# GEGLU after hash attention: weights staged in fp32 and cast on GpSimd, pair 0 in half-pair pieces, pairs 2 to 5 transposed by DMA

## Chip, cores and metric

One Trainium2 chip, one core of it. The metric is the device time of one execution in microseconds. The kernel before was run six times; an execution taken by the hardware profiler gives the trace that all stage times below come from.

## What is computed

Attention over 4 batches, 8 heads, 768 tokens and a head size of 64, in which a query sees only keys of the same hash bucket (six signs of a random projection), followed by a gated MLP on the heads laid side by side (512 columns):

```python
q_bits = np.einsum('bhsd,dk->bhsk', q, proj) > 0          # k_bits alike; six bits a token
mask = q_bucket[:, :, :, None] == k_bucket[:, :, None, :]
scores = np.where(mask, scale * q @ k.T, -1e9)
attn = softmax(scores) @ v                                # [4, 8, 768, 64]
x = attn.transpose(0, 2, 1, 3).reshape(B * S, H * D)      # [3072, 512]
ffn = (gelu(x @ w_gate) * (x @ w_val)) @ w_out            # d_ff = 1536
out = x + sigmoid(x @ w_res) * ffn
```

All inputs and the output are fp32; the kernel multiplies in bf16, and hashes in fp32.

## The kernel before

**Pairs, chunks and slots.** Heads go in pairs: 16 pairs, four to a batch. The scores of a pair are cut into nine chunks of 1024 columns (line 311): each has blocks of 128 keys by 512 or 2 x 256 queries for both heads. One chunk is one slot, and the main loop at line 575 has 144 of them. A slot issues the score matmuls of its chunk (`scores`, line 374) into one of two PSUM buffers `sp`, then ScalarE's exponential into `e` (line 378), then the tasks hung on that slot by `at(slot, f, ...)`, then in batches 1 to 3 some MLP matmuls as filler, and last the value matmuls of an earlier chunk (`flush`, `values`, line 355). The order on every engine is that of the program; nothing is reordered by a scheduler.

**Masks as extra rows.** Seven extra rows of q and k carry the hash bits, so that unequal buckets give a large negative score. The first head of a pair uses rows 0 to 71 of the transposed tile `aug`; the second head uses the tile `second`, whose rows 64 to 127 are a copy of `aug`'s (`move_second`, line 192, GpSimd) and whose rows 0 to 6 are the mask rows. Rows 7 to 63 are zero. The preparation of a pair is: `load` (line 88, SP's queue) of q, k and v in fp32; `cast` to bf16 (lines 175 to 179); a transpose on PE (line 200) with a copy out of PSUM (lines 206 and 208) or by DMA (line 187); `blocks` (line 212), VectorE's 32x32 transposes of the fp32 tile for the hash; `hash_half` (line 248, fp32 matmuls, then bits at line 253); `spread` (lines 261 and 268), which puts the bits in rows; and the mask rows. Pair 0's are copied in place by VectorE and ScalarE (`spread_in_place`, line 281); all others are moved by four small DMAs (`mask_rows`, line 290). `values_prep` (lines 293 to 308, GpSimd) casts v and sums it over the blocks of keys.

**Where each pair is prepared.** Pair 0 and most of pair 1 come ahead of slot 0 (lines 470 to 503). Pairs 2 and 3 are prepared in slots 1 to 14, transposed on PE, hashed together (two halves of 384 columns). From pair 4 on, two pairs are prepared at a time in the 18 slots before they are needed, transposed by DMA.

**The MLP.** In the fourth slot of the next batch (`LEAD = 4`), `gate_val` (line 383) computes 12 blocks of 128 hidden columns: eight matmuls with `wg`, GELU on ScalarE (line 399), eight with `wv`, a product on VectorE (line 402). `project` (line 407) is the filler of the rest of the batch: `wr` and tanh (lines 415 and 418), `wo` (line 425), the end on VectorE and GpSimd (lines 430 and 432). A planner gives each slot of batches 1 to 3 so many filler matmuls that PE's load is even; batch 0 has no filler.

**The weights.** `load_w` (line 162) issues a DMA on GpSimd that reads fp32 and writes bf16. The weights come in 12 pieces: eight quarters of `wg` and `wv`, `wr`, and three thirds of `wo`. Four are issued in slots 17 to 20, the other eight in slot 39, just ahead of the first gate stage.

## Time and profile before

| what | us |
|---|---|
| median of six runs (lowest to highest) | 363.06 (361.79 to 364.22) |
| the profiled execution | 363.67 |
| its span in the trace | 361.9 |
| first exponential starts | 12.75 |
| gate matmuls of batch 0 begin | 58.0 |
| last gate stage begins | 306.2 |
| PE busy in the span | 348.6 (96%) |
| ScalarE busy in the span | 211.8 (59%) |
| VectorE busy in the span | 147.1 (41%) |
| GpSimd busy in the span | 123.7 (34%) |

The profile gives, for groups of instructions, a line of the kernel, the engine, what is written and read, the count, the busy time, the mean of one in ns, and the idle time ahead of them with what ended it. A timeline lists start and duration in us, and in brackets the idle time before an instruction and its releaser. A table of windows gives, for each stretch, busy time and count of PE, PE's weight loads, VectorE, ScalarE and GpSimd, then the granted share of PE's clock, the share of the 16 DMA engines that was busy, and GB/s. PE's busy time is modelled from the start of matmuls, so a busy PE need not be at its peak. SP only issues DMAs; a DMA that waits for its data in SP's queue holds up all that stand behind it.

### The profile page before, as it was taken

What the parts mean: (1) busy time and instruction counts of PE and PEld (TensorE: products, weight loads), DVE (VectorE), ACT (ScalarE), POOL (GpSimd) and SP (SyncE); (2) the same over time, 40 slices, a digit from 0 to 9 for tenths busy, and PEclk for the clock granted to TensorE, in tenths of its full rate; (3) what the DMA queues carried; (4) which work ended last, traced back from release to release, by engine and by line L of the source; (5) the groups of instructions that cost most, each with busy time, mean ns of one, the idle gap of its engine ahead of it and who ended that gap; (6) DMA issues with size and microseconds to landing.
All of it is one profiled execution on the core that took longest, in us unless ns stands there. A gap on an engine that the chain in (4) does not pass through costs nothing.

```text
span 361.9 us, 7467 instructions
## 1 busy us (share of the span) xinstructions
PE 348.6 (96%) x3078; PEld 203.4 (56%) x3078; DVE 147.1 (41%) x200; ACT 211.8 (59%) x234; POOL 123.7 (34%) x178
## 2 busy tenths in 40 slices
PE   8897999999999999999999999999999999999994
PEld 3555565665465566566455556656555655666442
DVE  7764544333344334434343434334442123333343
ACT  4787797234788787232877777332778885232210
POOL 7997079100448258300046547400025112000000
PEclk9999899999999999999999999999999999999999
DMA  7569988997206942830005954510002210000012
GB/s 248 191 203 183 272 151 135 191 269 123 74 7 162 209 144 83 210 121 0 2 4 139 157 214 114 124 37 2 1 2 77 66 51 31 29 2 0 31 60 85
DMA packets 50201, 38.02 MB, mean 105 GB/s; under 512 B 28244, under 2 KB 47096, under 8 KB 50168
## 3 DMA queue, kind: packets, MB, share of 16 engines
q1 hardware_dynamic: 43752, 32.31, 33.6%
q0 software_dynamic: 6336, 5.24, 9.6%
q8 instruction: 24, 0.39, 0.4%
q14 instruction: 9, 0.07, 0.1%
q10 hardware_dynamic: 80, 0.00, 0.0%
HBM read 29.36 MB, written 6.29 MB: 99 GB/s over the span
## 4 chain that ended last, share of the span: by engine, by line
PE 86%; DMA 5%; POOL 3%; ACT 2%; DVE 2%; issue 1%; SPq 0%; DVEq 0%; POOLq 0%; ACTq 0%
PE sp L393 34%; PE fps L425 17%; PE sp L374 14%; PE av L355 8%; PE rps L415 5%; PE hs L248 3%; DMA ld<-in_q_dram 2%; DMA ldv<-in_v_dram 2%; PE av L348 2%; ACT e L378 1%; DMA second<-bits 1%; PE spr L261 1%; POOL second L192 1%; POOL nat L177 1%; ACT th L418 1%
## 5 line engine op out<-in xcount | busy, mean ns | idle before, releaser
L378 ACT ACTIVATE e<-sp 128x1024 bf16<-128x1024 f32 x144 | 144.8, 1024 | 38.2 <-PE sp L374 36.3
L399 ACT ACTIVATE gt<-sp 128x768 bf16<-128x768 f32 x48 | 38.9, 811 | 82.9 <-PE sp L393 82.9
L402 DVE SCALAR_TENSOR_TENSOR hh<-gt,sp 128x768 bf16<-128x768 bf16 x48 | 45.8, 954 | 81.7 <-PE sp L393 81.7
L425 PE MATMUL fps<-wo,hh 128*128 128x512 bf16 x288 | 75.4, 378 | 0.0
L432 POOL TENSOR_TENSOR o<-o,x_tok 128x512 f32<-128x512 f32 x18 | 20.8, 1156 | 148.0 <-DVE o L430 76.7
L393 PE MATMUL sp<-x_sb,wg 128*128 128x512 bf16 (+1 forms) x384 | 70.4, 326 | 0.1
L393 PE MATMUL sp<-x_sb,wv 128*128 128x512 bf16 (+1 forms) x384 | 70.2, 326 | 0.0
L355 PEld LDWEIGHTS <-e 128*128 128x128 bf16 x1152 | 52.2, 98 | 30.8 <-issue 9.5
L355 PE MATMUL av<-va,e 128*128 128x65 bf16 x1152 | 58.7, 194 | 0.6 <-ACT e L378 0.5
L374 PE MATMUL sp<-second,second 128*128 128x512 bf16 x192 | 55.4, 329 | 1.9 <-DMA second<-bits 1.9
L374 PE MATMUL sp<-aug,aug 71*128 71x512 bf16 x192 | 55.3, 328 | 1.3 <-ACT e L378 1.0
L393 PEld LDWEIGHTS <-wg 128*128 128x128 bf16 x384 | 37.4, 98 | 24.9 <-issue 0.3
L393 PEld LDWEIGHTS <-wv 128*128 128x128 bf16 x384 | 37.4, 98 | 24.5
L425 PEld LDWEIGHTS <-hh 128*128 128x128 bf16 x288 | 27.6, 97 | 27.6
L430 DVE SCALAR_TENSOR_TENSOR o<-th,fps 128x512 f32<-128x512 f32 x24 | 16.4, 684 | 56.2 <-PE fps L425 51.5
L192 POOL COPY second<-aug 64x768 bf16<-64x768 bf16 x32 | 25.9, 826 | 29.4 <-DMA aug<-nat 18.0
L212 DVE STREAM_TRANSPOSE t<-ld 128x768 f32<-128x768 f32 x32 | 29.5, 952 | 0.0
L415 PE MATMUL rps<-wr,x_sb 128*128 128x512 bf16 x96 | 24.6, 379 | 0.0
L418 ACT ACTIVATE th<-rps 128x512 f32<-128x512 f32 x24 | 14.3, 594 | 16.3 <-PE rps L415 13.0
L374 PEld LDWEIGHTS <-second 128*128 128x128 bf16 x192 | 18.8, 98 | 7.6 <-DMA second<-bits 2.4
L268 DVE CAST bits<-spr 128x512 bf16<-128x512 f32 (+1 forms) x23 | 15.4, 679 | 12.5 <-PE spr L261 11.6
L374 PEld LDWEIGHTS <-aug 71*128 71x128 bf16 x192 | 16.3, 98 | 4.2 <-issue 1.0
(56 smaller groups left out, 216.3 us busy)
## 6 DMA issues: line engine op xcount, KB each, us to landing
ld<-in_q_dram SPq DMA_DIRECT2D x16, 384.0 KB
ld<-in_k_dram SPq DMA_DIRECT2D x16, 384.0 KB
ldv<-in_v_dram SPq DMA_DIRECT2D x16, 384.0 KB
out_dram<-o SPq DMA_DIRECT2D x24, 256.0 KB
wg<-in_moe_w_gate_dram POOLq DMA_DIRECT2D x4, 384.0 KB, 6.8
wv<-in_moe_w_val_dram POOLq DMA_DIRECT2D x4, 384.0 KB, 9.0
wo<-in_moe_w_out_dram POOLq DMA_DIRECT2D x3, 512.0 KB, 22.5
wr<-in_moe_w_res_dram POOLq DMA_DIRECT2D x1, 512.0 KB, 16.0
```

Source lines behind the costliest of these rows:

```text
L192: eng.tensor_copy(second[x[0] % NM][x[1]][D:P], aug[x][D:P])
L212: nc.vector.transpose(tt.rearrange("p c h n -> p (c h n)"), raw[x].rearrange("p c d -> p (c d)"))
L355: nc.tensor.matmul(o[:, qt, :], e[:, off:off + P], va[:, hi, jt, 0:D + 1], start=False, stop=(jt == T - 1), skip_group_check=True)
L374: nc.tensor.matmul(sp[:, off:off + nq * P], ks[0:n, jt, :], qs[0:n, qt0:qt0 + nq, :], start=True, stop=True)
L378: nc.scalar.activation(e, sp, AF.Exp, scale=float(ALPHA))
L393: nc.tensor.matmul(sp[:, c0:c1], w[:, kk, bass.ts(m, P)], xs[:, kk, c0:c1], start=(kk == 0), stop=(kk == KM - 1))
L399: nc.scalar.activation(gt, sp[:, 0:S], AF.Gelu)
L402: nc.vector.scalar_tensor_tensor(hh[:, m, :], gt, 0.5, ps[1][:, 0:S], op0=ALU.mult, op1=ALU.mult)
L415: nc.tensor.matmul(rps, x_sb[b][:, kk, t, :], wr[:, kk, :], start=(kk == 0), stop=(kk == KM - 1))
L418: nc.scalar.activation(th, rps, AF.Tanh, scale=0.5)
L425: nc.tensor.matmul(fps, hh[:, m, bass.ts(t, P)], wo[:, m, :], start=(m == 0), stop=(m == KF - 1))
L432: last.tensor_add(o3, o3, x_tok[b][:, :, t, :])
```

## The change

- The weights come as fp32 over SP's queue into two staging buffers `ws` of 128x1536, and GpSimd casts them into place (`load_w`, `cast_w`). There are 14 pieces: the eight quarters, two halves of `wr`, four quarters of `wo`. Four are loaded and cast in the slots of pairs 2 and 3; two more are loaded at the first slot of batch 1, and at its second slot the rest follow, cast and load in turn.
- Pair 0 is cut into 12 chunks of 768 columns, six for one head and then six for the other. q and k of its first head are loaded first, by SP and by ScalarE's queue, ahead of `proj`. Its casts, block transposes, hashes, spreads and mask copies are done by head. Those of the second head are moved into slots 0 to 2. There are 147 slots; `base(p)` is the first slot of pair p.
- Pair 1 is prepared in slots 0 to 8 and still transposed on PE. Two of its four mask-row DMAs are issued by GpSimd.
- Pairs 2, 3, 4 and 5 are cast earlier and transposed by DMA from SP; pairs 2 and 3 are hashed singly, and their values are summed on GpSimd. The loads are placed anew.
- The warm-up has seven matmuls, on a smaller tile, in place of nine, two, three and two. The zero fill of `second` for pairs 2 and 3 and the selector for merged pairs move into slots; the ones in the value tiles are set by VectorE.
- From pair 6 on, slots and order are as before.

```diff
+    ws_pool = ctx.enter_context(tc.tile_pool(name="ws", bufs=2))
...
+    load(0, (0,), heads=slice(0, 1))
+    load(0, (1,), nc.scalar, heads=slice(0, 1))
     nc.scalar.dma_start(proj_sb, proj)
-    load(0, (0, 1))
...
+    load(0, (0, 1), heads=slice(1, 2))
...
+    warm = const.tile([P, P], BF16, name="warm")
+    nc.vector.memset(warm, 0.0)
...
+    load(0, (2,))
     load(1, (0, 1))
-    load(0, (2,))
...
+    sels = {}
+    def make_sel(i):
+        sides = ((0, 0, 1, 1), (0, 1, 0, 1))[i]
...
+        sels[i] = sel
+    make_sel(0)
...
-    for pair in second:
-        for t in pair:
+    def zero_second(i):
+        for t in second[i]:
             nc.vector.memset(t[0:D], 0.0)
+    zero_second(0)
+    zero_second(1)
...
-        nc.gpsimd.memset(va[:, :, :, D:D + 1], 1.0)
-        nc.gpsimd.memset(vsum[:, :, D:D + 1], float(T))
+        nc.vector.memset(va[:, :, :, D:D + 1], 1.0)
+        nc.vector.memset(vsum[:, :, D:D + 1], float(T))
...
+    wload, staged = [], []
...
-    wload.append((wr, moe_w_res.rearrange("(o p) n -> p o n", p=P)))
-    for s in range(3):
-        n = KF // 3
-        wload.append((wo[:, s * n:(s + 1) * n],
-                      moe_w_out[s * n * P:(s + 1) * n * P].rearrange("(o p) n -> p o n", p=P)))
+    for w, ap, n in ((wr, moe_w_res, 2), (wo, moe_w_out, 3)):
+        for o in range(0, w.shape[1], n):
+            wload.append((w[:, o:o + n],
+                          ap[o * P:(o + n) * P].rearrange("(o p) n -> p o n", p=P)))
     def load_w():
-        if wload:
-            nc.gpsimd.dma_start(*wload.pop(0))
+        dst, src = wload.pop(0)
+        st = ws_pool.tile([P, 3 * DMODEL], FP32, tag="ws", name="ws")
+        st = st[:, 0:dst.shape[1] * dst.shape[2]].rearrange("p (o n) -> p o n", o=dst.shape[1])
+        nc.sync.dma_start(st, src)
+        staged.append((dst, st))
+    def cast_w():
+        nc.gpsimd.tensor_copy(*staged.pop(0))
...
-            nc.tensor.matmul(wps, eps_sb, warm, start=True, stop=True)
-    def cast(x, eng=nc.gpsimd):
+            nc.tensor.matmul(wps, warm, warm.unsqueeze(1).to_broadcast([P, 4, P]),
+                             start=True, stop=True)
...
+    def transposed_head(x, h, eng):
+        rows = slice(D * h, D * h + D)
+        dst = second[x[0] % NM][x[1]] if h else new_aug(x)
+        (nc.scalar.copy if eng is nc.scalar else eng.tensor_copy)(dst[rows], tps[x][rows])
...
-    def blocks(x):
-        tt = t32_pool.tile([P, HT, 2, 32], FP32, tag="t32", name="t32")
-        nc.vector.transpose(tt.rearrange("p c h n -> p (c h n)"),
-                            raw[x].rearrange("p c d -> p (c d)"))
-        t32[x] = tt
+    def blocks(x, c0=0, c1=HT):
+        if x not in t32:
+            t32[x] = t32_pool.tile([P, HT, 2, 32], FP32, tag="t32", name="t32")
+        nc.vector.transpose(t32[x][:, c0:c1].rearrange("p c h n -> p (c h n)"),
...
-    def blocks(x):
-        tt = t32_pool.tile([P, HT, 2, 32], FP32, tag="t32", name="t32")
-        nc.vector.transpose(tt.rearrange("p c h n -> p (c h n)"),
-                            raw[x].rearrange("p c d -> p (c d)"))
-        t32[x] = tt
+    def blocks(x, c0=0, c1=HT):
+        if x not in t32:
+            t32[x] = t32_pool.tile([P, HT, 2, 32], FP32, tag="t32", name="t32")
+        nc.vector.transpose(t32[x][:, c0:c1].rearrange("p c h n -> p (c h n)"),
...
+    head_chunks = [[(h, 0, jt, 0, 4), (h, 512, jt, 4, 2)] for h in range(2) for jt in range(T)]
+    pair_chunks = []
     for i in range(T // 2):
-        chunks += [[(2 * i, 0, 4)], [(2 * i + 1, 0, 4)], [(2 * i, 4, 2), (2 * i + 1, 4, 2)]]
-    NCH = len(chunks)
+        for parts in ([(2 * i, 0, 4)], [(2 * i + 1, 0, 4)], [(2 * i, 4, 2), (2 * i + 1, 4, 2)]):
+            pair_chunks.append([(h, 512 * h + 256 * j) + part
+                                for h in range(2) for j, part in enumerate(parts)])
...
-    warm_up(9)
-    cast((0, 0), nc.scalar)
+    H0, H1 = slice(0, 1), slice(1, 2)
+    warm_up(7)
     for dh in range(2):
         for a in range(4):
-            copy = (nc.scalar.copy, nc.gpsimd.tensor_copy)[dh]
+            copy = (nc.vector.tensor_copy, nc.gpsimd.tensor_copy)[dh]
             copy(projw[32 * a:32 * a + 32, dh, NBITS * a:NBITS * (a + 1)],
-                            proj_sb[32 * dh:32 * dh + 32])
+                 proj_sb[32 * dh:32 * dh + 32])
+    for x, c0, c1 in (((0, 0), 0, T), ((0, 1), 0, T), ((0, 0), T, HT)):
+        blocks(x, c0, c1)
+    for h in (H0, H1):
+        cast((0, 0), nc.scalar, h)
+        cast((0, 1), nc.gpsimd, h)
+    transpose_pe((0, 0), TP)
+    for dh in range(2):
+        hash_half((0, 0), dh, SC)
+    transpose_pe((0, 1), AV)
+    transposed_head((0, 0), 0, nc.vector)
+    transposed_head((0, 1), 0, nc.scalar)
+    spread_in_place((0, 0), (SC, SC))
+    blocks((0, 1), T, HT)
+    values_prep(0)
     for side in range(2):
-        blocks((0, side))
-    cast((0, 1))
-    transpose_pe((0, 0), TP)
-    transposed((0, 0), nc.scalar)
-    warm_up(2)
+        transposed_head((0, side), 1, nc.vector)
+        cast((1, side))
+    load(1, (2,))
+    load(3, (0, 1))
     for dh in range(2):
-        hash_half(0, dh, ROW)
-    transpose_pe((0, 1), AV)
-    transposed((0, 1), nc.scalar)
-    move_second((0, 0))
-    cast((1, 0))
-    move_second((0, 1))
-    spread_in_place(0)
-    load(3, (0, 1))
-    load(1, (2,))
-    cast((1, 1))
-    values_prep(0)
-    warm_up(3, ROW)
-    transpose_pe((1, 0), ROW)
-    transposed((1, 0), nc.scalar)
+        at(0, hash_half, (0, 1), dh, ROW)
+    at(1, blocks, (1, 0))
+    at(2, spread_in_place, (0, 1), (ROW, SC))
+    at(2, blocks, (1, 1))
     for side in range(2):
-        blocks((1, side))
-    warm_up(2, AV)
-    transpose_pe((1, 1), AV)
-    transposed((1, 1), nc.vector)
+        at(1 + side, cast, (2, side))
+        at(2 + side, transpose_dma, (2, side))
+        at(6 + side, cast, (3, side))
+        at(8 + side, transpose_dma, (3, side))
+        at(2 + side, transpose_pe, (1, side), (TP, ROW)[side])
+        at(3 + side, transposed, (1, side), nc.vector)
+        at(4 + side, move_second, (1, side))
+    for dh in range(2):
+        at(4, hash_half, 1, dh, TP)
+    at(5, spread, 1, 0, 4, ROW)
+    at(6, spread, 1, 4, T, TP)
+    at(6, mask_rows, 1, (nc.sync, nc.gpsimd))
+    at(8, values_prep, 1)
+    at(4, zero_second, 2)
+    at(base(1) + 4, zero_second, 3)
     for side in range(2):
-        at(0, move_second, (1, side))
+        at(7, blocks, (2, side))
+        at(9 + side, move_second, (2, side))
+        at(base(1) + side, blocks, (3, side))
+        at(base(1) + side, move_second, (3, side))
     for dh in range(2):
-        at(0, hash_half, 1, dh)
-    at(1, spread, 1, 0, 4, ROW)
-    at(2, spread, 1, 4, T, TP)
-    at(2, mask_rows, 1)
-    at(8, values_prep, 1)
+        at(10 + dh, hash_half, 2, dh, ROW)
+        at(base(1) + 5 + dh, hash_half, 3, dh, ROW)
+    at(base(1) + 2, spread, 2, 0, 4, TP)
+    at(base(1) + 3, spread, 2, 4, T, ROW)
+    at(base(1) + 3, mask_rows, 2)
+    at(base(1) + 3, values_prep, 2)
...
+    at(base(1) + 7, spread, 3, 0, 4, TP)
+    at(base(1) + 8, spread, 3, 4, T, ROW)
+    at(base(1) + 8, mask_rows, 3)
+    at(base(1) + 6, values_prep, 3)
+    at(4, load, 4, (0, 1))
+    at(5, load, 2, (2,))
+    at(base(1), load, 5, (0, 1))
+    at(base(1) + 3, load, 3, (2,))
+    for side in range(2):
+        at(base(1) + 2 + side, cast, (4, side))
+        at(base(1) + 4 + side, transpose_dma, (4, side))
+        at(base(1) + 4 + side, cast, (5, side))
+        at(base(2) + side, transpose_dma, (5, side))
+        at(base(1) + 8, move_second, (4, side))
+        at(base(2) + 6, move_second, (5, side))
+        for i in range(2):
+            at(base(2) + 2 + 2 * i + side, blocks, (4 + i, side))
+        at(base(2) + 7 + side, hash_half, 4, side)
+    at(base(2), make_sel, 1)
+    for i, s in enumerate((0, 2, 3)):
+        at(base(3) + s, spread, 4, 4 * i, 4 * i + 4)
+    at(base(3) + 3, mask_rows, 4)
+    at(base(3) + 6, mask_rows, 5)
+    at(base(3), values_prep, 4)
+    at(base(3) + 6, values_prep, 5)
+    at(base(2) + 1, load, 4, (2,))
+    at(base(2) + 6, load, 5, (2,))
+    at(base(3) + 4, load, 6, (0, 1))
+    at(base(3) + 5, load, 7, (0, 1))
+    at(base(3) + 6, load, 6, (2,))
...
     for i in range(4):
-        x = (2 + i // 2, i % 2)
-        at(1 + i, cast, x)
-        at(2 + i, blocks, x)
-        at(4 + i, transpose_pe, x, (ROW, TP)[i % 2])
-        at(4 + i, transposed, x, nc.vector)
-        at(5 + i, move_second, x)
...
-    for dh in range(2):
-        at(8 + dh, hash_half, 2, dh, ROW)
-    for i, s in enumerate((10, 11, 12)):
-        at(s, spread, 2, 4 * i, 4 * i + 4, (TP, ROW, TP)[i])
-    at(12, mask_rows, 2)
-    at(14, mask_rows, 3)
-    for p in (2, 3):
-        at(6 * p - 2, values_cast, p)
-        at(3 * p + 8, values_sum, p, nc.vector)
-    at(4, load, 2, (2,))
-    at(5, load, 4, (0, 1))
-    at(7, load, 3, (2,))
-    at(8, load, 5, (0, 1))
-    at(16, load, 4, (2,))
-    for p in range(4, NPAIR, 2):
-        s0 = NCH * (p - 2)
+        at(base(2) + (3, 3, 13, 13)[i], load_w)
+        at(base(2) + (4, 5, 14, 16)[i], cast_w)
+    for p in range(6, NPAIR, 2):
...
-            at(s0 + (8 if p == 4 else 4) + i // 2, transpose_dma, x)
-            at(s0 + (11 if p == 4 else 8) + i, move_second, x)
+            at(s0 + 4 + i // 2, transpose_dma, x)
+            at(s0 + 8 + i, move_second, x)
...
-    for s in [17, 18, 19, 20] + 8 * [39]:
-        at(s, load_w)
+    for i in range(2):
+        at(base(4), load_w)
+    for i in range(8):
+        at(base(4) + 1, cast_w)
+        at(base(4) + 1, load_w)
+    for i in range(2):
+        at(base(4) + 1, cast_w)
...
+        if p == 0:
+            flush(2)
+        elif c != (1 if ends else 2):
```

## The prediction

> **What bounds the kernel now.** I read the stages first, then ScalarE's exponentials within the first stage, then what they wait for. Cutting the span at the first exponential (12.75), where the gate matmuls of batch 0 begin (58.10), at the first projection (90.20) and at the last gate stage (306.20), the table of stages says, in columns of busy time and count by engine, then clock and DMA:
>
> ```profile
> 0.00:12.75 12.75, 9.93 (x82) 4.70 (x86) 9.66 (x18) 6.67 (x11) 10.05 (x34) 1.00 0.86 286
> 12.75:58.10 45.35, 41.11 (x547) 26.44 (x536) 25.91 (x39) 38.02 (x41) 31.08 (x43) 0.96 0.81 178
> 58.10:90.20 32.10, 32.10 (x212) 19.36 (x209) 11.47 (x13) 12.62 (x15) 6.58 (x9) 1.00 1.08 188
> 90.20:306.20 216.00, 214.34 (x1967) 125.41 (x1966) 80.37 (x108) 141.18 (x152) 75.25 (x94) 1.00 0.33 85
> 306.20:361.90 55.70, 51.10 (x282) 27.51 (x281) 19.73 (x24) 13.31 (x18) 0.74 (x1) 1.00 0.09 34
> ```
>
> After 58.10 PE is busy 297.54 of 303.80 us: only fewer or faster matmuls shorten that, and the change leaves them. Before 58.10 ScalarE is the engine to watch, 38.02 of 45.35 us. The line of the exponential, asked for up to 70 us, and ScalarE's timeline show how its 40 instructions lie (36 of batch 0, 4 of the next, ahead of the gate stage):
>
> ```profile
> L378 ACT ACTIVATE e<-sp x40: 1017/1024/1055, 12.8 to 58.0; 128x1024 bf16<-128x1024 f32 x40
> ...
>   PE sp L374: 7.2, 12
> ```
>
> ```profile
> 12.75 4.94 ACT L378 ACTIVATE e<-sp 128x1024 bf16<-128x1024 f32 x5
> ...
> 22.63 1.02 ACT L378 ACTIVATE e<-sp 128x1024 bf16<-128x1024 f32 x1 [0.54 <-PE sp L374]
> 24.20 2.90 ACT L378 ACTIVATE e<-sp 128x1024 bf16<-128x1024 f32 x3 [0.54 <-PE sp L374]
> ...
> 34.58 1.94 ACT L378 ACTIVATE e<-sp 128x1024 bf16<-128x1024 f32 x2 [1.90 <-PE sp L374]
> ...
> 57.99 1.02 ACT L378 ACTIVATE e<-sp 128x1024 bf16<-128x1024 f32 x1 [0.55 <-PE sp L374]
> ```
>
> Five in a row take 4.94, so the pitch is (4.94 - 1.02)/4 = 0.98 us. The stage is 12.75 (start) + 40 x 0.98 = 39.1 + 7.2 (12 waits for scores) = 59.0, where the last one ends; the gate matmuls begin 0.9 before that. Everything the change can win lies in these three terms. The longest wait, 1.90, is a mask-row transfer of pair 2, as the waits of that stretch name it, and the clock falls in the window after it:
>
> ```profile
> PE sp L374 <- DMA second<-bits: 1.9, 1, 1.9
> ```
>
> ```profile
> 31.52:34.93 3.41, 1.44 (x20) 0.74 (x17) 0.27 (x1) 1.51 (x3) 2.34 (x3) 1.00 1.03 150
> 34.93:38.34 3.41, 3.41 (x24) 1.90 (x22) 2.56 (x4) 3.17 (x4) 0.00 (x0) 0.50 1.25 219
> ```
>
> The DMA share is 1.03 there: GpSimd's casting weight loads (issued from 27.32 on) lie in front of the mask rows. The first exponential itself waits for a serial chain: q lands at 4.02, cast, transpose, hash, spread, and mask copies that end at 12.03 because ScalarE's two at line 281 wait for GpSimd's move, which stands behind a cast of pair 1 whose load comes late (from the timeline of the start); a copy of pair 1 (0.80) follows them on ScalarE:
>
> ```profile
> 8.67 0.83 POOL L177 TENSOR_SCALAR nat<-ld 128x768 bf16<-128x768 f32 x1 [1.33 <-DMA ld<-in_q_dram]
> ...
> 9.57 0.82 POOL L192 COPY second<-aug 64x768 bf16<-64x768 bf16 x1
> ...
> 10.43 0.79 ACT L281 CAST aug<-spr 7x768 bf16<-7x768 f32 x1 [2.10 <-POOL second L192]
> ```
>
> **What the Trainium skill says.** "ScalarE: Activation LUTs", section "What ACT_TABLE_LOAD costs": an activation with immediate scale takes 186 ns plus 0.833 ns an element, and neighbours overlap by about 93 ns. Estimates from it: 1039 ns for 1024 columns (the trace: 1024), pitch 946 (trace: 980). For 768 columns I use the trace, 811 ns (the GELU row of that width), less the measured overlap of 45 ns: 0.77 us pitch. "TensorE: Matmul & The Clock Gate", Part 1: the clock is set by a free-running window of 3.413 us and falls to half after an idle one. The trace agrees on size (34.93 to 38.34) but fell with 1.44 of 3.41 busy, not idle; 2.31 of 3.42 busy (7.62 to 11.04) did not. "DMA: Bandwidth & Descriptors", "Anatomy of one DMA": a fixed 2.0 us besides the bytes. The first q load, 3.28 us from issue to use with the k load interleaved, fits: two loads of 0.39 MB at the 370 to 390 GB/s of the windows of 3 to 12 us are 2.1 us. "GPSIMD Engine Reference", "Engine selection": a one-input operation runs there at roughly line rate; the trace has 0.82 us for 128x768.
>
> **The change, part by part.**
>
> *Start, head by head.* Half loads of q (SP) and k (ScalarE's queue) should land by 3.7, the second halves by 4.8. The small proj load now stands behind the k half; its first use before was 4.54 behind other work, so I put it at 4.2 (3.97 to 4.6). VectorE then does four proj copies (0.4, from 0.18 each on GpSimd, overlapped), and three half block transposes of 0.48 (half of 0.957): 4.6, 5.1, 5.6, 6.1. GpSimd's copies (0.85) and k casts (2 x 0.43) end at 5.95. PE transposes q (0.35 to 0.5) at 5.35, hashes head 0 with half the columns (0.45, half of 0.86) to 6.2, transposes k to 6.65, spreads to 7.0. ScalarE's copy of k (0.80 for this width) ends at 7.5; its two half-width mask copies (0.79/2 each) end at 8.35; VectorE's end at 8.1. Scores 0.4: first exponential at 9.0 against 12.75, **3.75 gained**; bounds 8.3 (proj early) and 10.2 (everything one load of 1.03 us later). Moving small memsets to VectorE adds 8 x 0.07; two pairs of zero fills (4 x 0.4) move behind the first slots. The shorter warm-up costs nothing unless the clock drops (rival below).
>
> *Pair 0 in 12 chunks of 768.* 12 x 0.77 = 9.2 instead of 9 x 0.98 = 8.8: 0.4 lost. The mask copies of head 1 on ScalarE, formerly ahead of the first exponential, now stand among them: 2 x 0.40 = 0.8 lost. Together **1.2 lost**. PE needs 0.5 a chunk (6 of 8 of 0.24 for values and 0.75 of 0.43 for scores), so it follows.
>
> *Waits in the stage.* The 1.90 and its clock effect (0.24 at 36.77) go: weights come over SP in fp32 later, at slot base(2)+3, and pair 2's mask rows are issued six slots ahead. The 0.33 at 18.02 goes with PE transposes of pairs 2 and 3 (they go to SP's queue, 1.3 us of issue each). The two 0.54 stand at halves of the merged hash (0.75 us of PE against 0.98 - 0.68 = 0.30 spare in a slot); with pairs hashed singly four halves of 0.38 stay, about 0.1 each: 0.7 gained. Kept: 7.2 less 1.90, 0.24, 0.33 and 1.08 is 3.6, plus 0.4, is 4.0. New: pair 1's mask rows, ready at about 16.8 on VectorE's count, stand on SP behind two transposes, the two loads of pair 4 (0.79 MB) and v of pair 2 (0.39 MB), 3.1 us of DMA; they land between 18.8 and 21.3, wanted at about 20.2: 0 to 2.5 including GpSimd, whose value sums for pair 1 follow its two mask DMAs (0.8 each) and end near 22.0, wanted at 22.5. I take 1.0, and 0.3 for the clock. New sum 5.3 against 7.2: **1.9 gained**.
>
> *Weights.* Fourteen pieces: 12 of 1536 columns at 2 x 0.82 = 1.64 us of GpSimd, and 2 of 1024 at 1.1, 21.9 us in all, instead of 12 issues of 0.8. Four lie in batch 0, where GpSimd has 14.3 of 45.35 us free: nothing for the end. Ten stand in front of the gate stage: two buffers, each cycle 2.0 (fixed) + 2.1 (0.79 MB) + 1.64 = 5.8 us for two pieces, 2.9 a piece. From 49 on they end at 75 to 79. The gate stage needs its third quarter 15 us after its start (68) and the projection 32 us after (85): free by 6 us. Queued behind the casts on GpSimd are the casts of pair 7, and behind the loads on SP the transposes of pairs 6 and 7; these belong to slots after the gate stage, and pair 6 is used 14 slots later. GpSimd is idle from 64.7 to the end of this stage now, so the cover is real.
>
> *Sum.* -3.75 + 1.2 - 1.9 = **-4.4**. Against the profiled execution (363.67, span 361.90) that gives 359.3; that run lies 0.6 above the median of 363.06, and the same saving from the median gives **358.7**. Later stages keep their 303.8.
>
> **Rivals.**
> *B, waits vanish.* Pair 1's mask rows arrive in time, proj is early, and the smaller hash halves fit fully: start 8.5, waits 3.8: -0.5 - 1.5 more, 356.7. For: SP's mask rows took about a microsecond each in an empty queue; against: loads lie ahead.
> *C, a new wait in place of the old.* Pair 1's masks 2.5 late, and PE, about 1.9 of 3.4 us busy before the first exponential, falls to half clock at its start: 3.4 us in which a chunk needs 1.0 instead of 0.77, some 1.3 with the preparation. Saved 4.4 - 1.5 - 1.3 + the 0.3 already taken: 1.9; 361.2.
> *D, slower: the weights come late.* If each two-buffer cycle took 9.6 us instead of 5.8, as when fp32 loads share the engines (1.08 share in that stage now) and GpSimd is held up, ten pieces from 49 end at 97, 12 after the projection wants them (85), though its twelve matmuls read the last piece late: about 9 lost, less 4.4: 367.7. It decides from 3.9 us a piece; at 4.3 all is lost again. Against: DMA moved 280 GB/s and more where only fp32 loads were queued.
>
> **How the numbers follow.** Forecast 0.52 (own range 357.5 to 360.4), B 0.16, C 0.20, D 0.12. The range 355.6 to 362.8 takes in B with its low bound and C with 1.6 more; D and a small tail are out. About 0.3%, 1.1 us, can be told from no change: below 362.0 lie the forecast, B and half of C, 0.78; within, 0.10; slower, D, 0.12.
>
> **What would show it.** First exponential at 8.3 to 10.2; 12 of 768 columns near 0.81 us; total wait before exponentials 4 to 6.5, none over 1 except at pair 1; first gate matmul near 53.7; from there to the end still 303.8. A gap of PE at line 393 or at the first projection would show D; a clock of 0.50 before 15 us or a wait for mask rows near 20 shows C. The forecast is wrong if the first exponential is not earlier by 2.5, or if the part after the first gate matmul grows.

## The result, and the profile after

The kernel after takes **367.34 us** (median, 363.66 to 370.17) against 363.1 for the kernel before beside it: a ratio of 1.0101, 95% interval [1.0078, 1.0124], about 1% slower. The prediction said 358.7, with 355.6 to 362.8 as its range. The medians take all executions, the ratio only those within 1.5% of the fastest of their kernel, which leaves out four of the 17 here and the profiled one. That one took 369.37 (span 367.58), 2.0 more than the median, so the sums below, made in spans, are larger than the 3.7 us that the ratio stands for. What they rest on, waits for `wo` and half clock after them, stands in the traces of e2 and e15 too, whose executions count in their ratios; PE's waits in e15 begin with

```profile
PE fps L431 <- POOL wo L168: 3.4, 2, 2.6
```

The table of stages, cut at the first exponential, the first gate matmul, the first projection and the first matmul of the last gate stage, for the kernel after:

```profile
0.00:10.56 10.56, 7.53 (x49) 3.62 (x53) 6.85 (x27) 4.06 (x6) 7.16 (x22) 1.00 0.83 275
10.56:57.76 47.20, 43.68 (x578) 28.30 (x579) 27.52 (x48) 39.07 (x44) 31.52 (x44) 1.00 0.76 198
57.76:90.01 32.25, 32.25 (x216) 19.47 (x213) 11.63 (x14) 12.74 (x15) 17.95 (x16) 1.00 0.79 249
90.01:310.80 220.79, 216.28 (x1962) 125.55 (x1961) 79.20 (x106) 141.28 (x152) 79.38 (x97) 0.98 0.37 99
310.80:367.58 56.78, 52.24 (x291) 28.08 (x288) 20.88 (x26) 13.31 (x18) 1.16 (x1) 0.98 0.09 33
```

The earlier table's cuts at 58.10 and 306.20 are not quite these events: in the trace of the kernel before, the first gate matmul starts at 57.97 and the last gate stage at 304.98. Cut there, the fourth line of the kernel before reads

```profile
90.22:304.98 214.76, 213.18 (x1961) 124.82 (x1960) 79.20 (x106) 141.16 (x152) 74.83 (x93) 1.00 0.33 86
```

The start is 2.2 shorter, the next stage 2.0 longer (before, 57.97 - 12.75 = 45.2), so the gate matmuls begin where they did, and a stage that the change was not to touch, from the first projection to the last gate stage, is longer by 6.0 us (220.79 - 214.76). There the clock column no longer reads 1.00 (the 0.98 of the last line belongs to the last 2 us of the span, in which PE has no work left). PE's timeline at the first projection says why:

```profile
90.87 1.46 PE L455 MATMUL fps<-wo,hh 128*128 128x512 bf16 x6
93.16 0.81 PE L455 MATMUL fps<-wo,hh 128*128 128x512 bf16 x3 [0.83 <-POOL wo L177]
...
96.58 1.44 PE L455 MATMUL fps<-wo,hh 128*128 128x512 bf16 x3 [2.17 <-POOL wo L177]
```

The last two pieces of `wo` aren't cast when PE wants them. In the window in which PE waits, its busy time falls to 1.28 of 3.41, and the two windows after it run at half clock:

```profile
92.30:95.71 3.41, 1.28 (x8) 0.67 (x7) 0.25 (x1) 1.02 (x1) 1.46 (x2) 1.00 1.06 292
95.71:99.12 3.41, 2.54 (x7) 0.90 (x7) 0.69 (x1) 0.21 (x1) 2.60 (x4) 0.50 0.25 51
99.12:102.53 3.41, 3.41 (x22) 1.22 (x20) 0.00 (x0) 2.03 (x3) 3.35 (x5) 0.50 0.79 198
```

The price, as an estimate: 0.83 + 2.17 of waiting, and (6.83 - 0.87 of that wait)/2 = 3.0 for half clock, 6.0 in all. From the end of the last of the 40-odd exponentials ahead of the gate stage to the end of the kernel it is 302.89 before and 308.78 after, 5.9 more. I call this length **the tail** below, and the time of that exponential's end **L** (59.01 before, 58.80 after).

GpSimd's timeline shows the weights, casts in place of casting DMAs; SP's timeline (after "SPq") shows their loads:

```profile
50.07 1.47 POOL L177 CAST wv<-ws 128x1536 bf16<-128x1536 f32 x1 [1.97 <-DMA ws<-in_moe_w_val_dram]
...
59.63 1.47 POOL L177 CAST wg<-ws 128x1536 bf16<-128x1536 f32 x1 [3.51 <-DMA ws<-in_moe_w_val_dram]
...
63.84 1.47 POOL L177 CAST wv<-ws 128x1536 bf16<-128x1536 f32 x1
...
66.98 1.47 POOL L177 CAST wg<-ws 128x1536 bf16<-128x1536 f32 x1
70.08 1.47 POOL L177 CAST wv<-ws 128x1536 bf16<-128x1536 f32 x1 [1.64 <-DMA ws<-in_moe_w_val_dram]
...
95.06 1.47 POOL L177 CAST wo<-ws 128x1536 bf16<-128x1536 f32 x1 [1.95 <-DMA ws<-in_moe_w_out_dram]
```

```profile
49.65 1.48 SPq L315 DMA_DIRECT2D aug<-bits  x2
51.19 0.44 SPq L88 DMA_DIRECT2D ld<-in_q_dram  x1
51.68 0.45 SPq L88 DMA_DIRECT2D ld<-in_k_dram  x1
52.24 0.41 SPq L173 DMA_DIRECT2D ws<-in_moe_w_gate_dram  x1
52.77 0.43 SPq L173 DMA_DIRECT2D ws<-in_moe_w_val_dram  x1
```

The third and fourth piece are issued at 52.2 and 52.8, behind pair 4's mask rows and the loads of pair 6, with those of pair 7 after them; their casts start at 59.63 and 63.84, the second behind pair 5's values on GpSimd. The first buffer is free after the first of these casts, the second only after the other, at 65.3: the ten late pieces run from 61.72 (first issue) to 96.5 (last cast's end), 34.8 us. Pair 4's first exponential, whose slot holds the first of them, came near 53.3.

### The profile page after: what moved, and what is told of

The parts are those of the page before. It is cut to its first block, busy times and chain, and to the rows that moved or that the text cites. A ratio compares the mean times of both kernels' runs of the same rounds, so it can differ in the third digit from the quotient of the medians.

```text
span 367.6 us, 7520 instructions
## 1 busy us (share of the span) xinstructions
PE 352.0 (96%) x3081; PEld 205.0 (56%) x3081; DVE 146.1 (40%) x217; ACT 210.5 (57%) x234; POOL 137.2 (37%) x179
## 4 chain that ended last, share of the span: by engine, by line
PE 74%; DMA 12%; POOL 6%; DVE 3%; ACT 2%; issue 1%; SPq 1%; ACTq 0%; DVEq 0%; POOLq 0%
PE sp L423 25%; PE fps L455 16%; PE sp L404 13%; PE av L386 7%; PE rps L445 5%; DMA ws<-in_moe_w_val_dram 5%; PE hs L273 3%; DMA ws<-in_moe_w_out_dram 3%; POOL wv L177 2%; PE spr L286 1%; DMA ws<-in_moe_w_gate_dram 1%; ACT e L408 1%; PE av L381 1%; DMA ldv<-in_v_dram 1%; DMA ws<-in_moe_w_res_dram 1%
## 5 line engine op out<-in xcount | busy, mean ns | idle before, releaser
L408 ACT ACTIVATE e<-sp 128x1024 bf16<-128x1024 f32 (+1 forms) x147 | 145.0, 1008 | 44.5 <-PE sp L404 42.8
L455 PE MATMUL fps<-wo,hh 128*128 128x512 bf16 x288 | 76.2, 381 | 3.0 <-POOL wo L177 3.0
L404 PE MATMUL sp<-aug,aug 71*128 71x512 bf16 x192 | 56.3, 338 | 2.6 <-ACT e L408 1.1
L208 POOL COPY second<-aug 64x768 bf16<-64x768 bf16 x30 | 24.2, 827 | 20.1 <-DMA aug<-nat 14.5
L236 DVE STREAM_TRANSPOSE t<-ld 128x768 f32<-128x768 f32 (+1 forms) x34 | 29.8, 907 | 0.1
L445 PE MATMUL rps<-wr,x_sb 128*128 128x512 bf16 x96 | 25.5, 389 | 0.0
```

Of the source, the lines that this page charges most:

```text
L208: eng.tensor_copy(second[x[0] % NM][x[1]][D:P], aug[x][D:P])
L236: nc.vector.transpose(t32[x][:, c0:c1].rearrange("p c h n -> p (c h n)"), raw[x][:, c0:c1].rearrange("p c d -> p (c d)"))
L404: nc.tensor.matmul(sp[:, off:off + nq * P], ks[0:n, jt, :], qs[0:n, qt0:qt0 + nq, :], start=True, stop=True)
L408: nc.scalar.activation(e[:, 0:n], sp[:, 0:n], AF.Exp, scale=float(ALPHA))
L445: nc.tensor.matmul(rps, x_sb[b][:, kk, t, :], wr[:, kk, :], start=(kk == 0), stop=(kk == KM - 1))
L455: nc.tensor.matmul(fps, hh[:, m, bass.ts(t, P)], wo[:, m, :], start=(m == 0), stop=(m == KF - 1))
```

## Experiments

Theories go by letters in the texts on record, with the mechanism in words. Behind each median stands the ratio to the kernel before, run beside it, with its 95% interval. e1 to e3, e6 to e10, e12 to e14, e17 and e18 start from the kernel after, e4, e5, e11, e15 and e16 from the kernel before. Where a version is named as another one with an edit added, only an edit that is new is shown, or its first line if it was shown already.

### Weights, warm-up, or neither

**e1, the kernel after with weights by casting DMAs again** (twelve pieces issued by GpSimd, four early, eight at the gate stage):

```diff
-        nc.sync.dma_start(st, src)
-        staged.append((dst, st))
+        nc.gpsimd.dma_start(*wload.pop(0))
...
-        at(base(2) + (3, 3, 13, 13)[i], load_w)
-        at(base(2) + (4, 5, 14, 16)[i], cast_w)
+        at(base(2) - 1 + i, load_w)
```

> The changed kernel, with the weights loaded as before: 12 casting DMAs issued by GpSimd, no staging buffers and no casts of weights. Theory W (the two-buffer chain of load and cast ends late; PE waits 0.83 and 2.17 us for the last pieces of wo, its clock halves from 95.7 to 102.5, and the values of pair 5 wait behind a weight cast, 1.2 us): these go, 3.0 + about 3 + 1.2, so 360 to 361 us, clearly faster than before, with the time from the first gate matmul to the end back at 304. Theory C (what is lost is lost at the start, where PE runs at half clock until 17.2 us): 366 to 367, little changed.

Measured: 365.37, ratio 1.0055 [1.0033, 1.0076]; L 60.37, tail 303.15. The tail is back to that of the kernel before, so staging makes the end late; but L is 1.6 later than in the kernel after, as pair 4's mask rows, now behind the casting DMAs, are waited for (2.3 at 54.1). The time lies between what the two theories said.

**e2, the kernel after with a longer warm-up**, and **e3, both edits together**:

```diff
-    warm_up(7)
+    warm_up(9)
...
     transpose_pe((0, 0), TP)
+    warm_up(2, ROW)
...
     spread_in_place((0, 0), (SC, SC))
+    warm_up(3, ROW)
```

> The changed kernel, with nine warm-up matmuls in place of seven and two and three more in PE's gaps before the first exponential. Theory C: PE has full clock by 8 us, the first exponential comes at 9.3 instead of 10.56 and the five waits of 0.6 to 0.8 us among the first chunks of 768 go, together 3 to 4 us; since the weights' chain hangs on mask rows that follow the exponentials, it moves with them: 363.5 to 364.5. Theory W alone: the start is earlier but the last piece of wo lands when it did, so 367 and a longer wait of PE at the first projection.

> Both edits: casting DMAs for the weights and the longer warm-up. If W and C are two separate losses: 356.5 to 358, near the forecast for the change. If one contains the other: no more than 1 us below the better of the two single edits.

Measured: 368.3, 1.0139 [1.0097, 1.0181], and 365.82, 1.0074 [1.0046, 1.0102]. The first exponential comes at 9.62 instead of 10.56, and the waits of 0.74 to 0.82 in pair 0 shrink to 0.18; but ScalarE's timeline (of e2) has a new one at pair 1's first exponential, for its mask rows:

```profile
20.60 0.81 ACT L408 ACTIVATE e<-sp 128x768 bf16<-128x768 f32 x1 [0.27 <-PE sp L404]
23.79 1.02 ACT L408 ACTIVATE e<-sp 128x1024 bf16<-128x1024 f32 x1 [2.38 <-PE sp L404]
```

In e2 L is 58.35, 0.45 earlier, and the tail is 310.03, with 4.7 of waits for `wo`; in e3 L is 60.90, after a wait of 3.65 for the same mask rows, and e3 is not faster than e1. The clock at the start isn't what makes the kernel slow.

**e4, the kernel before with seven warm-up matmuls alone**, and **e5, the kernel before with staging alone**:

```diff
-    warm_up(9)
+    warm_up(7)
...
-    warm_up(2)
...
-    warm_up(3, ROW)
...
-    warm_up(2, AV)
```

> The kernel before, with only seven warm-up matmuls and none of the later two, three and two. Theory C: PE stays at half clock well past 10 us here too, and the kernel loses 2 to 4 us: 365 to 367. If the shorter warm-up is harmless: 362.5 to 363.5.

```diff
+    ws_pool = ctx.enter_context(tc.tile_pool(name="ws", bufs=2))
...
-            nc.gpsimd.dma_start(*wload.pop(0))
+        nc.sync.dma_start(st, src)
+        staged.append((dst, st))
...
-    for s in [17, 18, 19, 20] + 8 * [39]:
+    for i in range(4):
+        at(18 + (3, 3, 13, 13)[i], load_w)
+        at(18 + (4, 5, 14, 16)[i], cast_w)
```

> The kernel before with the weights part of the change alone: 14 fp32 pieces over SP into two buffers, cast by GpSimd, at the slots that stand for those of the change. Theory W: the time from the first gate matmul to the end grows from 303 to about 309, and in exchange pair 2's mask rows no longer queue behind casting DMAs (1.9 us of wait and the half clock after it): 366 to 368. If the weights only cost together with the rest of the change: 362 to 364.

Measured: e4 364.2, 1.0024 [1.0004, 1.0043], with L as before (59.08) though the first exponential comes at 11.83. That isn't the work of the shorter warm-up: in e5, e11, e15 and e16, whose instructions ahead of slot 0 are those of the kernel before, it comes at 11.64 to 12.08, and pair 1's at 21.58 to 22.03, as here of e5:

```profile
11.64 1.03 ACT L384 ACTIVATE e<-sp 128x1024 bf16<-128x1024 f32 x1
...
21.58 1.02 ACT L384 ACTIVATE e<-sp 128x1024 bf16<-128x1024 f32 x1 [0.54 <-PE sp L380]
```

The 12.75 of the one trace of the kernel before is a late start; there a cast of pair 1 on GpSimd waits 1.33 for its load, in e5 not at all. e5 took 363.41, 1.0016 [0.9995, 1.0038]. Staging as such doesn't make the kernel slow. In e5 the wait of 1.90 ahead of pair 2 is gone:

```profile
26.85 8.46 ACT L384 ACTIVATE e<-sp 128x1024 bf16<-128x1024 f32 x9 [0.79 <-PE sp L380]
...
52.18 1.02 ACT L384 ACTIVATE e<-sp 128x1024 bf16<-128x1024 f32 x1 [1.57 <-PE sp L380]
```

but one of 1.57 stands at pair 4. Its ten late pieces take 34.7 us, as in the kernel after, but their first issue is at 56.1 instead of 61.7: the last cast ends at 90.8, 1.2 after `wo`'s first matmul (89.65), and PE doesn't wait. In the kernel after it ends 5.7 after (90.87).

### Fewer staged pieces on the kernel after, and pair 1's mask rows

**e6, eight late pieces by casting DMAs**, **e7, e6 with the warm-up**, **e8, e7 with two loads behind pair 1's mask rows**:

```diff
-    for i in range(2):
-        at(base(4), load_w)
...
     for i in range(8):
-        at(base(4) + 1, cast_w)
-        at(base(4) + 1, load_w)
...
+        at(base(4) + 3, load_w_cast)
```

> The changed kernel with its four staged pieces in batch 0 kept, and the other eight pieces loaded by casting DMAs at the last slot before the gate stage, as before. Theory W: what follows the first gate matmul is back at 303, and unlike with casting DMAs throughout, pair 4's mask rows don't queue behind them (2.3 us there): about 362.5 to 363.5. Rival: the four pieces in batch 0 cost as much as the ten: 365 or more.

```diff
-    warm_up(7)
+    warm_up(9)
```

> The same with the longer warm-up. With casting DMAs the longer warm-up brought an earlier first exponential (9.8) but pair 1 then waited 3.65 us for its mask rows. Theory M (pair 1's mask rows, on SP behind two transposes and three loads, set the end of pair 0 whatever PE's clock): within 0.5 us of the run without the longer warm-up. Theory C (clock): 3 us less.

```diff
-    at(4, load, 4, (0, 1))
-    at(5, load, 2, (2,))
+    at(7, load, 4, (0, 1))
+    at(7, load, 2, (2,))
```

> As the run before, and the loads of pair 4 and of v of pair 2 moved from slots 4 and 5 to slot 7, behind pair 1's mask rows. Theory M: the wait ahead of pair 1 falls from about 2.4 to 3.6 us to under 1, and the kernel gains 2 to 3 us on it: 360 to 361. If the rows wait for the hash or for the transposes in SP's queue and not for the loads: no gain.

Measured: 367.94, 1.0143 [1.0097, 1.0188]; 369.63, 1.0181 [1.0125, 1.0237]; 367.01, 1.0115 [1.0069, 1.0162]. None helped; the tails are 307.0, 308.0 and 306.3. In e6 the DMAs are issued on GpSimd only at 67, behind the staged casts and pair 5's values, and now the gate stage itself waits (1.9 for `wv`) and the projection too (1.7 for `wo`). In e7 the wait for `wv` is 2.4. In e8 pair 1's first exponential comes at 21.87:

```profile
20.68 0.81 ACT L411 ACTIVATE e<-sp 128x768 bf16<-128x768 f32 x1 [0.27 <-PE sp L407]
21.87 3.77 ACT L411 ACTIVATE e<-sp 128x1024 bf16<-128x1024 f32 x4 [0.38 <-PE sp L407]
```

against 23.44 in e7, with SP's mask rows issued at 17.38 in both: the loads of 1.18 MB ahead of them are what held them, by 1.6. L, though, is 57.72 against 56.89, as PE waits 2.1 for pair 4's value sum later.

### Everything bulky earlier

**e9, loads of pairs 6 and 7 earlier (kernel after)**, **e10, e9 with the warm-up and pair 1's masks first**:

```diff
-    at(base(3) + 4, load, 6, (0, 1))
-    at(base(3) + 5, load, 7, (0, 1))
+    at(base(2) + 5, load, 6, (0, 1))
+    at(base(2) + 8, load, 7, (0, 1))
```

> The changed kernel, with the q and k loads of pairs 6 and 7 moved from the end of batch 0 (four and five slots into pair 3) to the slots of pair 2, where the kernel before has them. Theory Q (it is the start of the weights' chain, not its speed, that is late: pieces three and four stand in SP's queue behind 0.8 MB and beside 1.6 MB of these loads; the chain from the second quarter's first cast to wo's last takes 36 to 37 us in the changed kernel and in the kernel before with staged weights, but starts at 59.6 against 54.7): the first of those casts comes at 54 to 56, the last of wo ends near 92, what follows the last exponential of the lead falls from 308.8 to about 304, and the kernel takes 362.5 to 364.5. If the chain's speed is to blame: 366.5 to 368.

```diff
-    at(4, load, 4, (0, 1))
+    at(7, load, 4, (0, 1))
```

> The same, with the longer warm-up and the loads of pair 4 and of v of pair 2 behind pair 1's mask rows. Theories Q, M and C as separate losses: another 1 to 2.5 us off, 360.5 to 363. If staging sets the end whatever happens earlier: as the run before.

**e11, e5 with weight loads earlier**, **e12, e10 with weight loads earlier**:

```diff
-        at(18 + (3, 3, 13, 13)[i], load_w)
-        at(18 + (4, 5, 14, 16)[i], cast_w)
+        at(18 + (-2, -2, 4, 4)[i], load_w)
+        at(18 + (1, 3, 8, 11)[i], cast_w)
...
-        at(36, load_w)
+        at(32 + i, load_w)
```

> The kernel before with staged weights, the pieces loaded and cast earlier (six loaded before the first slot of batch 1, two of them 2 slots before pair 2's successors are prepared). Staged weights at the slots of the change gave 363.4, with the last cast of wo at 90.8, just when it was wanted. Theory Q: with some 4 us in hand the late cases go: 361 to 362.5. Otherwise 363 to 364.

```diff
-        at(base(2) + (3, 3, 13, 13)[i], load_w)
+        at(base(2) + (-2, -2, 4, 4)[i], load_w)
```

> As the second of this group, with the pieces loaded and cast earlier too. If the weights still set the end there: 359 to 361. If it is the attention of batch 0 that sets it: within 0.7 us of that run.

Measured: 366.64, 1.0089 [1.0054, 1.0123]; 366.88, 1.0094 [1.0059, 1.0129]; 369.66, 1.0171 [1.0138, 1.0204]; 367.72, 1.0124 [1.0073, 1.0176]. The tail is short in all four (302.8 to 303.8), and L is late (61.2, 61.2, 65.1, 64.0). A late L helps the tail: in e9 the last cast of `wo` ends 1.4 earlier than in the kernel after (95.1), but its first matmul also comes 2.4 later (93.25). The largest of PE's waits, of e9 and of e11:

```profile
PE sp L404 <- DMA aug<-bits: 4.3, 2, 3.6
```

```profile
PE sp L380 <- DMA aug<-bits: 6.9, 1, 6.9
```

The stretch from 41 to 60 holds the weights, the loads of two pairs, and mask rows on one queue. In e11 the bits of pair 4 are ready at 46.9, and their first mask row is issued at 53.72, behind two transposes and three loads: what goes ahead of the mask rows was paid for there.

### One load out of that stretch

**e13, load 7 among the late weights (kernel after)**, **e14, e13 with the warm-up and pair 1's masks first**, **e15, e5 with load 7 among them**:

```diff
-    at(base(3) + 4, load, 6, (0, 1))
-    at(base(3) + 5, load, 7, (0, 1))
+    at(base(2) + 5, load, 6, (0, 1))
...
         at(base(4) + 1, load_w)
+        if i == 3:
+            at(base(4) + 1, load, 7, (0, 1))
```

> The changed kernel, with the q and k loads of pair 6 moved to the slots of pair 2 (0.79 MB) and those of pair 7 (0.79 MB) into the middle of the ten staged pieces ahead of the gate stage, so that neither stands near pair 4's mask rows or in front of pieces three and four. Theory V (what moves the end is the volume that SP's queue and the DMA engines have to pass in order between 41 and 60 us: mask rows of pair 4, loads of pairs 6 and 7 and four pieces of weights; moving one part ahead only makes another late): with 2 us of DMA taken out, pair 4 starts at 53 to 54 where the run with both loads early had 55.8, the last cast of wo ends by 93, and the kernel takes 363 to 365. If it is the two staging buffers alone: 366 to 368 as the change.

```diff
-    warm_up(7)
+    warm_up(9)
```

> The same, with the longer warm-up and the loads of pair 4 and v of pair 2 behind pair 1's mask rows. Theory V: pair 1 starts at 21.9 and pair 4 at 51 to 53, the weights end in time, 361 to 363. If whatever is won earlier is always given back at the weights: as the run before.

```diff
-            at(s0 + 8, load, p + 3, (0, 1))
+            if p > 4:
+                at(s0 + 8, load, p + 3, (0, 1))
...
+        if i == 3:
+            at(37, load, 7, (0, 1))
```

> The kernel before with staged weights at the slots of the change, and the loads of pair 7 moved into the middle of the ten pieces. Theory V: pair 4 starts at 51 instead of 52.2 and the weights end 1 to 2 us earlier: 361 to 362.7. If that stretch is bound by the attention: as without the move, 363.4.

Measured: 364.52, 1.0058 [1.0028, 1.0087]; 365.24, 1.0063 [1.0036, 1.0089]; 365.79, 1.0078 [1.0048, 1.0109]. In e13 the tail is 302.76, L 60.07, and the time lies where its theory V had it. e14 and e15 miss theirs: in e14 L is 58.71, but PE waits 1.8 for `wo` (tail 304.7). In e15 L falls to 56.60, the best of the runs on the kernel before, but with the load in the chain the tail is 308.26, with 3.4 us of waits for `wo`.

### Six pieces taken out of the chain

**e16, e5 with `wr` and `wo` by casting DMAs**, **e17, the same on the kernel after**:

```diff
+    def load_w_cast():
+        nc.gpsimd.dma_start(*wcast.pop(0))
...
-    for i in range(8):
+    for i in range(2):
         at(37, cast_w)
         at(37, load_w)
+    for i in range(4):
+        at(37, load_w_cast)
```

> The kernel before with the fp32 staging for the eight quarters of wg and wv only; wr and wo go by GpSimd's casting DMAs, issued behind the third and fourth of the late casts. Theory V (a chain of ten pieces through two buffers at 3.3 to 3.5 us a piece is what comes late, and short bulk transfers ahead of the mask rows are what the staging is good for): the chain shortens to four pieces, all weights are in by 80 us, the part behind the gate stage's start stays 303, the exponentials before it end at 57.6 to 58: 361 to 363, up to 0.5% faster than before. Rival Z (what is won in the first 60 us by staging is given back somewhere else whatever the order of the weights): 363.5 to 365.

```diff
-    for i in range(8):
+    for i in range(2):
         at(base(4) + 1, cast_w)
         at(base(4) + 1, load_w)
+    for i in range(4):
+        at(base(4) + 1, load_w_cast)
```

> The changed kernel with the same: only the eight quarters of wg and wv staged, wr and wo by casting DMAs issued behind the third and fourth late cast. Theory V: no wait for wo, no half clock at the projections, the part behind the gate stage's start back from 308.8 to 303: 361.5 to 364. Rival P (GpSimd's own order, in which values and casts of pair 6 stand between the weight casts, delays the casting DMAs as well): waits at the first projection of 2 us or more stay, 366 to 368.

Measured: e16 362.87, 1.0000 [0.9980, 1.0020]; e17 363.56, 1.0014 [0.9994, 1.0034]. e17 settles the tail. There the chain starts as late as in the kernel after (first late issue 60.9), GpSimd's order is the same, but the chain has four pieces instead of ten, and the rest is under way by 74:

```profile
69.66 1.47 POOL L181 CAST wv<-ws 128x1536 bf16<-128x1536 f32 x1 [1.45 <-DMA ws<-in_moe_w_val_dram]
71.07 0.86 POOL L178 DMA_DIRECT2D wr<-in_moe_w_res_dram  x1
71.93 2.25 POOL L178 DMA_DIRECT2D wo<-in_moe_w_out_dram  x3
```

PE doesn't wait for a weight, and the table of stages has the line from the first projection to the last gate stage back at full clock, 6.0 us shorter than in the kernel after and as long as in the kernel before:

```profile
88.93:303.69 214.76, 213.19 (x1962) 124.80 (x1961) 79.20 (x106) 141.16 (x152) 74.75 (x93) 1.00 0.36 94
```

Neither is faster than the kernel before; the intervals reach 0.2% to either side.

**e18, e17 with the warm-up**:

```diff
-    warm_up(7)
+    warm_up(9)
```

> The changed kernel with wr and wo by casting DMAs (as the run before this one) and with a longer warm-up (nine matmuls ahead, then two, then three). Theory S (with the late weights gone, an earlier start is worth what it is worth): the first exponential a microsecond earlier, the exponentials before the gate stage end at 56.5 instead of 57.7, the rest stays 303: 362 to 362.8, 0.2% faster than before at best. Rival M (pair 1's mask rows take the earlier start back): end at 57.7 as without it, 363.5.

Measured: 364.06, 1.0028 [1.0007, 1.0048]. The first exponential is 1.2 earlier than in e17 (9.53 against 10.71), L 0.25 (57.47 against 57.72), for pair 1 waits 2.0 for mask rows. Even that quarter isn't seen in the median. No version beat the kernel before.

## Why the prediction was wrong

**The weights: the step that failed.** "From 49 on they end at 75 to 79 ... free by 6 us." They ended at 96.5. Two terms were off. The chain of ten began at 61.7 instead of 49: its slot came some 4 later (near 53.3), as the first stage gained nothing, and I left out that the third and fourth piece must be landed and cast before the buffers are free, which is the other 8.4, though I had counted these pieces ("nothing for the end"). And it took 34.8 us instead of 26 to 30, 3.1 us from cast to cast in the mean ((95.06 - 66.98)/9); the cast itself was shorter than I said, 1.47 against 1.64, and the loads took longer, 4.75 to 5.5 us from issue to cast (65.33 to 70.08, 71.58 to 77.06) against the 4.1 that I had put in. The 2.0 in that sum was weak: "DMA: Bandwidth & Descriptors", "Anatomy of one DMA", in the Trainium skill gives it for DMAs that GpSimd issues, these go by SP, and the check on the first q load doesn't bear it out (3.28 less 2.1 leaves 1.2). 12.7 late and 5 to 9 slower is what the margin of 6 could not hold, though the projection came at 90.0 instead of 85. I had argued from GpSimd's idle time; a chain of load, cast and next load through two buffers is bound by its latency, and idle time of the engine doesn't cover that. e17 shows the share: with the six pieces of `wr` and `wo` out of that chain the ratio falls from 1.0101 to 1.0014, 0.87 of a per cent or 3.2 us of the 3.7 that 1.01% are. Rival D named what would come late, and its 97 and 367.7 are close, but by luck. It had the chain start at 49 and go at 4.8 us a piece; it went at 3.1, less than the 3.9 from which D "decides", and the start did the greater part. And it priced the lateness at 9 (5.9 measured in the spans) and kept the gain of 4.4, which wasn't there.

**The start.** -3.75 said, -2.19 measured (10.56, outside my 8.3 to 10.2), and that against a late start: against the 11.64 to 12.08 of e5, e11, e15 and e16 it is -1.1 to -1.5. `proj` came at 4.66 on VectorE instead of 4.2, its four copies took 0.72 instead of 0.4; and PE was at half clock up to about 17.2: six transposes took 0.84 (at 13.25), and 0.50 in e2 after the longer warm-up. e2 puts the clock's share at 0.94 of the 1.6; over all traces the first exponential comes at 9.79 to 10.84 with the seven matmuls (six traces) and at 9.53 to 9.82 with the longer warm-up (eight). I had called the shorter warm-up free "unless the clock drops": here it didn't rise before 17.2.

**Pair 0.** +1.2 said; from its first exponential to pair 1's it was 13.96 against 9.88, +4.1. The pitch (0.4) and the two copies on ScalarE (0.96 against 0.8) were right. What I had left to rival C is the rest, 2.9 us more of waits (3.77 against 0.87):

```profile
12.11 1.51 ACT L408 ACTIVATE e<-sp 128x768 bf16<-128x768 f32 x2 [0.74 <-PE sp L404]
13.65 0.96 ACT L306 CAST second<-spr 7x384 bf16<-7x384 f32 x2
15.43 0.81 ACT L408 ACTIVATE e<-sp 128x768 bf16<-128x768 f32 x1 [0.82 <-PE sp L404]
17.03 0.81 ACT L408 ACTIVATE e<-sp 128x768 bf16<-128x768 f32 x1 [0.80 <-PE sp L404]
18.60 4.46 ACT L408 ACTIVATE e<-sp 128x768 bf16<-128x768 f32 x6 [0.76 <-PE sp L404]
```

The clock isn't all of it: with it repaired the waits move to pair 1's mask rows (e2, e18), and with those repaired as well (e8) pair 1 begins at 21.87, 0.8 before its time in the one trace of the kernel before, and no earlier than the 21.58 to 22.03 of the four with the same start. Twelve pieces and two copies use up the whole head start.

**The waits.** -1.9 said for all of them. They grew, from 7.2 to 8.6. Without those in pair 0 and at its end (0.87 before, 3.77 after, the latter put down above) and the one ahead of the first exponential (0.63), they fell from 6.3 to 4.2, and -2.1 is what the stretch from pair 1's first exponential to L lost: the 1.90 went, as I said, and the small ones fell from 4.4 to 2.8. At the end of the stage a new one of 1.45 came, which I hadn't seen: PE waits for pair 4's value sum on GpSimd (1.22), which stands behind a weight cast, at 50.07.

**The sum.** -2.2 + 4.1 - 2.1 + 5.9 = 5.7, the difference of the spans, against -4.4. "Later stages keep their 303.8" held for all that PE does, and failed for when its weights are there. Both signs that I had named for a wrong forecast came: the first exponential earlier by less than 2.5, and a longer part after the first gate matmul.

**What stays open.** Why e16 and e17, with L 1.0 and 1.3 earlier than in the kernel before and the same tail, show no gain in the median. Part of it may be the trace that they are compared with: its start is 0.7 to 1.1 later than in the four others, and its execution (363.67) lay 0.6 above the median, so L of the kernel before may be nearer 58.3 (an estimate: 59.0 less 0.7), and what is left, 0.3 to 0.6, is within the intervals. This isn't shown: I have one profiled execution of each, and e17's (362.65) lies near the lowest of its runs (362.08). What e6 and e8 lose beyond their spans is open for the same reason. Staging through more than two buffers was not run.

## What to carry to other kernels

A chain of load, cast and next load through two buffers has a pace of its own and a start that depends on whatever uses the buffers before it: work out when its first load can be issued, from the buffers and from all that stands ahead of it on the engine that issues and on the one that casts, before comparing its end with the time at which it is wanted. A head start at the beginning of a pipeline is worth only what the next stage's inputs can use: follow it to the next pair before adding it to a sum. One trace of the baseline can be off by what the sum is about: the start of the kernel before lay 0.7 to 1.1 us later in its trace than in four others with the same instructions. And where small DMAs that PE waits for share a queue with bulk loads, each bulk load moved earlier must be charged with the wait that it gives them.

## What the runs showed of the hardware

The clock. PE's windows before 17.2 in the kernel after were far from idle, and the clock still wasn't granted; they read

```profile
3.55:6.96 3.41, 2.35 (x22) 1.21 (x22) 2.17 (x7) 1.04 (x2) 1.68 (x6) 1.00 1.00 293
6.96:10.38 3.42, 2.44 (x24) 1.44 (x18) 2.55 (x6) 1.74 (x3) 3.18 (x5) 1.00 1.04 377
10.38:13.79 3.41, 3.41 (x35) 2.31 (x35) 2.72 (x6) 2.46 (x4) 2.65 (x4) 1.00 0.94 322
```

(the 1.00 of the clock column stands for no record yet; the durations, 0.83 for two matmuls of 512 columns at 14.56 against 0.49 at 18.01, show half clock). Here 2.4 of 3.4 busy wasn't enough to raise it, nor was the first window that was busy throughout; while in the kernel before 2.31 of 3.42 didn't lower it. PE's busy time is modelled, so no threshold is to be read from these figures. Nor is the same program granted the same clock each time: in e1, with the same seven warm-up matmuls, the first six transposes already ran at full clock. They are, in the kernel after and in e1:

```profile
4.97 0.82 PE L217 MATMUL tp<-ident,nat 128*128 128x128 bf16 x6 [0.81 <-ACT nat L192]
```

```profile
5.33 0.51 PE L212 MATMUL tp<-ident,nat 128*128 128x128 bf16 x6 [1.17 <-ACT nat L187]
```

In e1 the clock then fell at 7.74, after a window with 1.76 of 3.41 busy. "TensorE: Matmul & The Clock Gate", Part 1, in the Trainium skill speaks of an idle window; at 95.71 in the kernel after the clock fell after one with 1.28 busy, and there the measurement decides. Small DMAs behind bulk: pair 1's mask rows, issued on SP behind loads of 1.18 MB, were waited for by 2.4 us in e2, and moving those loads behind them took 1.6 us off (e7 against e8); at pair 4, behind two transposes and three loads, the wait was 6.9 us (e11).
